# Causal attention sums with the exponentials streaming through column tiles

## The chip, the cores and the metric

The kernel runs on one core of a Trainium2 chip. The metric is the device time of one execution in microseconds. Three timed executions of the kernel before took 1740.86, 1741.07 and 1743.66 us; the median, 1741.07 us, is the time before.

## The reference

Four attention layers follow each other on one sequence of 2048 tokens of width 512, with 32 heads of 16 dimensions: A, B, A, B. Each is added to its input, and each sees its input normalised.

```python
x = A_x
x = x + _A_ref(_layernorm(x), A_wq, A_wk, A_wv, A_wo, A_beta)
x = x + _B_ref(_layernorm(x), B_wqkv, B_wo)
x = x + _A_ref(_layernorm(x), A_wq, A_wk, A_wv, A_wo, A_beta)
x = x + _B_ref(_layernorm(x), B_wqkv, B_wo)
```

Layer A works on four segments of 512 tokens, with a causal softmax inside a segment and a memory carried from segment to segment; layer B is a plain softmax over all 2048 keys.

```python
# A, per segment s
logits = einsum('bhqd,bhkd->bhqk', qs, ks) * scale + mask      # causal, 512 x 512
a_dot = einsum('bhqk,bhkd->bhqd', softmax(logits), vs)
a_mem = (phi(qs) @ M) / (phi(qs) @ z + 1e-6)
o = g * a_mem + (1.0 - g) * a_dot
M, z = M + phi(ks).T @ vs, z + sum(phi(ks))
# B
o = softmax(q @ k.T * Dh ** -0.5) @ v
```

## The kernel before

A Python program writes out the order of all instructions of all engines. It simulates the engines' times as it goes and decides by them what comes next; wherever an engine needs another's result, the semaphore wait is derived from the buffers. The parameters of these decisions are class attributes (how late VectorE may be, how many banks it may take, and so on). `PLAN` overrides some of them for stretches of 40 units each: row k holds for units 40k to 40k + 39.

Layers are numbered 0 to 3; 0 and 2 are causal (A), 1 and 3 bidirectional (B). The attention work is cut into groups. A group is one segment of 512 queries, one chunk `c` of 8 heads, and every second head of it (`e` is 0 or 1), so four heads `r`. The masked queries `qm` hold the query rows of these heads with the others zeroed. Scores are computed transposed, keys on the partitions and queries in the 512 columns of a PSUM bank, in row tiles of 32 partitions that run side by side for the heads.

A causal group has three kinds of banks for each head, `k0`, `k13` and `k2`: the ten blocks of 128 keys by 128 queries on or below the diagonal, packed into whole banks (`PARTS`: key block, first column in the bank, columns, first query). The last kind is a half bank, and the pair's two groups (`e` = 0 and 1) share one bank for it (`k2`, `k2m`). So a pair has 20 banks. The triangle of the diagonal blocks is masked either on PE, by adding a matrix `tri` to the scores, or afterwards on POOL.

A unit takes three banks of scores; ACT exponentiates them together into `pT` (line 1643). Or it takes two, and one or two further banks (a "take", the code's `dx`) go to VectorE, which approximates the exponential in three parts by integer arithmetic: `dx_first` (line 1165) writes the first into `dxt` or into KA, QA, VA, wA or wB where those are idle, `task_dx` and `dx_four` (lines 1219 and 1236) the other two. A take has to be summed over keys three times. `TAKEN` and `TAKEN_A` limit the takes in a group, `REST` asks that so many banks still lie ahead, `R_NEAR`, `R_PAIRS`, `PAIRS` and `ACT1` say when a unit may take one or two; `ring_open`, `dx_open` and `dx_pick` read them.

Two units later the sums over keys follow (`pv_step`, `pv`), into one bank `sums` per group. In a group with `flip`, V of a head (16 columns and a column of ones, which gives the softmax's denominator) is the stationary operand and the 512 exponentials stream; the four heads use four column tiles of 32, so the sums come out with heads and features on the partitions and queries in the columns. Layers 1 and 3 do that, but for the last group. Causal groups have `flip` False: there each 128 x 128 block of exponentials is loaded as the stationary operand and V streams, 17 columns of it (`bcast` repeats them to 34 or 51 so that the write covers the bank), and the sums come out with queries on the partitions.

A group's end differs likewise. `finish` without `flip` takes the reciprocal (line 1732) and multiplies straight from PSUM into `ob` (line 1738). `finish_flip` copies the sums to `ub` (`evac`, line 561, or an addition where sums come in several waves, line 1767), has SP's queue transpose them into `tb`, and after both groups of a pair `divide` takes the reciprocal (line 1784) and multiplies into `ob`, on POOL by default (line 1788). From `ob` the queue transposes into `oT`, and the output projection (`task_out`) reads that. SP issues all transposes in order: `xT` from the normalised input `xn`, `phk` from the keys for the memory, `phq` from `amem`, `tb` and `oT`.

Projections, norms and the memory are background tasks, let in when PE is early against ACT; they use the bank `misc`, which takes use too. `mm_wide` splits a projection's matmul into four column tiles if the current group has `flip`. `keep_busy` and `fill_gaps` add matmuls with zeros (line 2032) where PE would be idle.

Causal groups come first wherever their inputs are ready; in layer 0 two segments can be in work at once, in layer 2 one.

Of the kernel before, what the change touches and what calls it, by code (L numbers as in the profile page):

```python
# [270 lines left out]

class Group:


    __slots__ = ("L", "kind", "qseg", "c", "e", "ksegs", "first", "last", "banks", "pos", "qm", "acc", "npv", "idx", "total", "started", "left", "taken", "shut", "mate", "flip", "begun", "dxr", "bank", "hold")

    def __init__(self, L, kind, qseg, c, e, ksegs, first=True, last=True):
# [22 lines left out]
        self.flip = kind == "B" and (L, qseg, c) != (3, NSEG - 1, NCH - 1)  # L300
        self.left = 40 if kind == "A" else (1 if self.flip else 4) * self.total
# [5 lines left out]
class Builder:  # L307
    STRETCH = 40
    PLAN = {
        0: dict(TAKEN_A=1, MASK_PE=800, PE_LOW=7, GAP=3, BG_BANK=400),  # L310
        1: dict(R_LATE=1200, BUSY_ROOM=300, CARRY_W=0, NEARW=40, PAIRS=999, LEVEL=3, TAKEN=0.5, DVE_LATE=1700, BUSY_BACK=800),
        2: dict(MARGIN=500, DX_BANK=900, NEAR=8, EARLY=300, FILL=0.42, CR_B=1200, PART=3, NEARW=20, PAIRS=60, DX_FIN=3000),
        3: dict(NEAR=8, TAKEN_A=1, PV_SKIP=900, BACK=8, CR_W=1900, NEARW=20, TAKEN=0.4, LOW=14, HOLD_AT=40, PHI_LATE=0),
        4: dict(R_LATE=1200, NEARW=40, PAIRS=24, LEVEL=3, TAKEN=0.5),
        5: dict(DX_LATE=700, SLACK=350, BACK=4, LEVEL=3, BUSY_WAIT=0, PE_LOW=7, DVE_LATE=1700),
        6: dict(NEAR=10, PV_SKIP=200, BACK=3, DX_LAG=3, MASK_PE=800, DIV_LATE=2500, BG_BANK=100, QUAD=0),
        7: dict(REST=10, SLACK=350, R_NEAR=10, EARLY=0, FILL_DVE=200, BUSY_ROOM=300, R_PAIRS=2, PAIRS=999, TAKEN=0.3, QWAIT=8, QMIN=4),
        8: dict(R_LATE=1200, BACK=2, CR_W=1300, NEARW=20, BUSY_WAIT=0, TAKEN=0.3, DVE_LATE=800, QWAIT=3, QMIN=4, HOLD_MAX=0, PHI_LATE=300),
        9: dict(ACT1=400, R_LATE=1200, DX_BANK=700, NEAR=18, CR_W=1900, CR_B=1800, R_PAIRS=2, PAIRS=24, DIV_LATE=800, DVE_LATE=800),
        10: dict(DX_LATE=500, NEAR=5, TAKEN_A=1, SLACK=250, CARRY_W=0, R_PAIRS=2, PAIRS=999, DIV_LATE=800, BUSY_WAIT=0, PE_LOW=4, DVE_LATE=800, BG_BANK=100, QUAD=0, HOLD_MAX=0, PHI_LATE=300),  # L320
        11: dict(DX_LATE=900, R_NEAR=10, BUSY_ROOM=900, FILL=0.42, OPART=4, MASK_PE=800, DIV_LATE=2500, DVE_LATE=800, QWAIT=3, QMIN=4, HOLD_SEGS=2, PHI_LATE=0, POOL_QM=1),
        12: dict(R_LATE=1200, BUSY_ROOM=900, FILL=0.4, OPART=4, LEVEL=3, TAKEN=0.4, DVE_LATE=800, QWAIT=8, QMIN=3, BUSY_BACK=1800),
        13: dict(MARGIN=350, DX_LATE=900, TAKEN_A=1, EARLY=300, CARRY_W=1500, PART=3, OPART=3, MASK_PE=800, GAP=3, QUAD=0, QWAIT=3, HOLD_SEGS=2),
        14: dict(ACT1=400, R_LATE=1200, DX_BANK=700, NEAR=18, CR_W=1900, CR_B=1800, PAIRS=24, DIV_LATE=800, DVE_LATE=800, PHI_LATE=300, DX_FIN=3000),
        15: dict(ACT1=400, MARGIN=400, EVAC_ACT=300, TAKEN_A=2, PV_SKIP=500, BUSY_ROOM=400, CR_A=1700, CARRY_W=400, PART=1, DX_LAG=3, DIV_LATE=800, DVE_LATE=800),
# [764 lines left out]
    def dx_pick(self, used):  # L1090
# [3 lines left out]
        for n, g in enumerate(self.sel):  # L1094
# [5 lines left out]
            for k in sorted(range(1, min(13 if isA else 9, len(g.banks) - g.pos + 1)), key=lambda k: g.dxr[g.banks[-k][1]]):  # L1100
                if g.banks[-k][1] not in used and g.banks[-k][0] != "k2":
                    bank = g.banks.pop(-k)
                    g.taken += 1
                    g.left += (1 if g.flip else 4) * len(EXP_STEPS)
                    g.dxr[bank[1]] += 1
                    for h in self.sel[:n]:
                        h.shut = True
# [989 lines left out]
```

## Time and profile before

| | |
|---|---|
| median of the timed executions | 1741.07 us |
| profiled execution | 1743.75 us, span 1742.0 us |
| instructions | 47805 |
| PE, ACT, VectorE (DVE), POOL busy | 95%, 98%, 88%, 10% of the span |
| mean granted TensorE clock | 0.998 of full |
| bytes moved by DMA | 54.60 MB, mean 31 GB/s |

The profile is one execution. PE's matmuls overlap, and their ends are modelled, so a busy PE isn't PE at its peak; the distance between the starts of matmuls says more. Nearly all matmuls are issued by one helper (line 522), so operands and shapes tell them apart, not lines. In a group's row stand its count, its busy time, the mean duration of one, and the idle time ahead of it with what ended that.

### The profile page before, as it was taken

The numbers are of one execution on the slowest core, as the hardware profiler recorded it, in microseconds if no ns is written. First come the engines' busy times: TensorE is split into PE (matmuls) and PEld (weight loads), VectorE is DVE, ScalarE is ACT, GpSimd is POOL, SyncE is SP. The second block draws the span as 40 slices with busy tenths as digits, with TensorE's granted clock in tenths as the row PEclk, the third lists the DMA queues.
The fourth block names the chain that finished last, engine by engine and source line by source line (L and its number), as shares of the span: only waits on it lengthen the run. The fifth ranks groups of instructions, "written<-read, shape, count | busy, mean of one in ns | idle before, by whom it ended". The sixth has DMA issues, their size and how long they took to land.

```text
span 1742.0 us, 47805 instructions
## 1 busy us (share of the span) xinstructions
PE 1652.7 (95%) x19946; PEld 604.6 (35%) x19946; DVE 1527.2 (88%) x2977; ACT 1703.7 (98%) x1608; POOL 182.8 (10%) x292
## 2 busy tenths in 40 slices
PE   8999899999999899999999999999999999999999
PEld 5553335332222523522235222532222222222236
DVE  6758665999999688799998999889999999999996
ACT  7899999999999999999999999999999999999998
POOL 2310100111100300100002100110010100000000
PEclk9999999999999999999999999999999999999999
DMA  6110211001221221102202111010011001000010
GB/s 176 37 22 20 44 14 29 17 8 22 41 47 23 56 56 32 33 8 59 59 14 38 46 32 41 19 46 14 10 23 26 22 13 23 10 10 11 8 29 18
DMA packets 148440, 54.60 MB, mean 31 GB/s; under 512 B 128768, under 2 KB 147712, under 8 KB 148224
## 3 DMA queue, kind: packets, MB, share of 16 engines
q1 hardware_dynamic: 148224, 51.56, 13.9%
q8 instruction: 156, 2.56, 0.6%
q14 instruction: 60, 0.49, 0.1%
HBM read 18.88 MB, written 2.10 MB: 12 GB/s over the span
## 4 chain that ended last, share of the span: by engine, by line
ACT 43%; PE 36%; issue 11%; DVE 6%; DMA 2%; SPq 1%; POOL 1%; ACTq 0%; DVEq 0%; POOLq 0%
ACT pT L1643 42%; PE ps L522 35%; PE ps L2032 1%; SPq L568 1%; DVE KA L1165 1%; DMA tb<-ub 1%; DMA xT<-xn 1%; POOL pT L1657 1%; DVE dxt L1165 1%; ACT amem L762 0%; DVE wA L1165 0%; DVE lnst L667 0%; POOL qm L1533 0%; DMA phq<-amem 0%; DVE VB L561 0%
## 5 line engine op out<-in xcount | busy, mean ns | idle before, releaser
L1643 ACT ACTIVATE pT<-ps 128x1024 bf16<-128x1024 f32 (+1 forms) x1561 | 1670.8, 1239 | 25.3 <-PE ps L522 19.4
L522 PE MATMUL ps<-qm,KB 32*128 32x512 bf16 x4096 | 571.0, 384 | 56.2 <-ACT pT L1643 43.7
L522 PE MATMUL ps<-pT,VB 128*17 128x512 bf16 x2907 | 497.4, 384 | 1.5 <-DVE QB L561 0.3
L522 PEld LDWEIGHTS ps<-qm,KB 32*128 32x128 bf16 x4096 | 148.4, 91 | 561.0 <-ACT pT L1643 462.0
L1165 DVE TENSOR_SCALAR KA<-ps 128x512 uint16<-128x512 f32 (+1 forms) x453 | 315.3, 704 | 11.4 <-PE ps L522 7.6
L1165 DVE TENSOR_SCALAR dxt<-ps 128x512 uint16<-128x512 f32 (+1 forms) x315 | 220.7, 704 | 12.5 <-PE ps L522 9.7
L522 PEld LDWEIGHTS ps<-pT,VB 128*17 128x17 bf16 x2907 | 116.6, 87 | 287.5 <-issue 274.3
L522 PE MATMUL ps<-dxt,VB 128*17 128x512 bf16 x939 | 197.5, 381 | 0.0
L2032 PE MATMUL ps<-woB,zero 128*32 128x512 bf16 (+7 forms) x655 | 166.9, 295 | 0.0
L522 PE MATMUL ps<-QA,VB 128*17 128x512 bf16 x445 | 129.5, 382 | 0.0
L1165 DVE TENSOR_SCALAR wA<-ps 128x512 uint16<-128x512 f32 (+1 forms) x174 | 123.2, 718 | 3.6 <-PE ps L522 1.1
L1788 POOL TENSOR_TENSOR ob<-tb,rd 128x512 bf16<-128x512 bf16 x31 | 35.7, 1152 | 817.9 <-DVE rd L1784 762.4
L522 PE MATMUL ps<-VA,VB 128*17 128x512 bf16 x445 | 120.3, 381 | 0.0
L1657 POOL TENSOR_SCALAR_AFFINE_SELECT pT<-pT 128x256 bf16<-128x256 bf16 (+4 forms) x113 | 61.7, 561 | 480.8 <-ACT pT L1643 480.8
L522 PE MATMUL ps<-KA,VB 128*17 128x512 bf16 x445 | 109.7, 381 | 0.0
L522 PE MATMUL ps<-wA,VB 128*17 128x512 bf16 x555 | 109.0, 381 | 0.0
L522 PE MATMUL ps<-VA,pT 128*128 128x51 bf16 (+1 forms) x2540 | 104.2, 187 | 4.7 <-POOL pT L1657 2.3
L522 PE MATMUL ps<-qm,KA 32*128 32x128 bf16 (+2 forms) x1536 | 93.1, 255 | 12.8 <-ACT pT L1643 9.4
L522 PEld LDWEIGHTS ps<-VA,pT 128*128 128x128 bf16 x2540 | 89.6, 96 | 23.2 <-issue 7.6
L1533 POOL TENSOR_SCALAR qm<-QB,par 128x512 bf16<-128x512 bf16 x96 | 74.0, 780 | 217.6 <-PE ps L522 197.7
L522 PE MATMUL ps<-woB,zero 128*32 128x512 bf16 (+1 forms) x282 | 92.7, 381 | 0.0
L1165 DVE TENSOR_SCALAR wB<-ps 128x512 uint16<-128x512 f32 (+1 forms) x109 | 81.2, 749 | 3.3 <-PE ps L522 2.4
(165 smaller groups left out, 1979.7 us busy)
## 6 DMA issues: line engine op xcount, KB each, us to landing
wB<-in_B_wqkv_dram SPq DMA_DIRECT2D x48, 128.0 KB, 2.3
wA<-in_A_wk_dram SPq DMA_DIRECT2D x16, 128.0 KB, 2.2
wA<-in_A_wq_dram SPq DMA_DIRECT2D x16, 128.0 KB, 2.4
wA<-in_A_wv_dram SPq DMA_DIRECT2D x16, 128.0 KB, 2.5
out_dram<-x SPq DMA_DIRECT2D x8, 256.0 KB, 2.2
x<-in_A_x_dram SPq DMA_DIRECT2D x3, 512.0 KB, 9.8
wB<-in_B_wqkv_dram SPq DMA_DIRECT2D x1, 1536.0 KB, 12.5
oT<-ob SPq DMA_TRANSPOSE x63, 2.4
```

Source lines behind the costliest of these rows:

```text
L522: self.sc.add("pe", lambda e: e.matmul(out, lhsT, rhs, start=start, stop=stop, skip_group_check=True), reads=reads, banks=[(bank, "w", all ...
L568: t[2] = self.sc.add_dma("sp", lambda e: e.dma_start_transpose(out, in_), b, reads=reads, writes=writes, deps=list(deps) + ([t[2]] if t[2] ...
L1165: self.op("dve", lambda e: e.tensor_scalar(d, o, SCALE * LOG2E * 128, 127.0 * 128 + EXP_BIAS, op0=ALU.mult, op1=ALU.add), writes=[self.b_d ...
L1533: self.op(eng, (lambda m, q, col: lambda e: e.tensor_scalar(m, q, col, 0.0, op0=ALU.mult, op1=ALU.add))(m, q, col), reads=[bq, self.b_par] ...
L1643: self.sc.add("act", (lambda dst, src: lambda e: e.activation(dst, src, ACT.Exp, scale=SCALE))(dst, src), writes=self.b_pT[slot * 3 + i:sl ...
L1657: self.op("pool", (lambda blk, pat: lambda e: e.affine_select(blk, blk, pattern=pat, compare_op=ALU.is_ge, fill=0.0, base=0, channel_multi ...
L1788: self.op(eng, lambda e: e.tensor_tensor(ob, t[:, :, :, 0:16], rb, ALU.mult), reads=[br] + self.b_tb, writes=self.b_ob[oi], **(dict(ns=125 ...
L2032: new = Op("pe", 0, (lambda o, z, w: lambda e: e.matmul(o, z, w, start=False, stop=False, skip_group_check=True))(o, z, w), f"fill {cols} ...
```

## The change

`Group.flip` becomes true for the causal layers in `FLIP_A`, both of them. Their sums run with V stationary and the exponentials streaming, in column tiles. `RUNS` lists for each kind of bank the runs of columns that share a key block and lie side by side in the queries: `k0` is one run of 512, `k13` three (256, 128, 128), `k2` one of 256. So a group has 20 summing matmuls, where it had 40. `pv_step` gathers the banks of one unit that belong to one group, and `pv_many` issues their runs in rounds: the first runs of all heads, then the second runs. `Group.sums` counts the matmuls of a bank. With `flip`, `finish` goes by `finish_flip`, and `mm_wide` and `keep_busy` use column tiles beside causal groups too. All rows of `PLAN` but the last are replaced.

```diff
+FLIP_A = (0, 2)
+RUNS = {"k0": [(0, 0, 512, 0)], "k13": [(1, 0, 256, 128), (1, 384, 128, 384), (3, 256, 128, 384)], "k2": [(2, 0, 256, 256)],
+        "k2m": [(2, 256, 256, 256)]}
...
+    def sums(self, what):
+        if self.kind == "A":
+            return len(RUNS[what]) if self.flip else 2 if what in ("k2", "k2m") else 4
+        return 1 if self.flip else 4
...
-        self.flip = kind == "B" and (L, qseg, c) != (3, NSEG - 1, NCH - 1)
-        self.left = 40 if kind == "A" else (1 if self.flip else 4) * self.total
+        self.flip = L in FLIP_A if kind == "A" else (L, qseg, c) != (3, NSEG - 1, NCH - 1)
+        self.left = sum(self.sums(w) for w in ("k0", "k13", "k2")) * 4 if kind == "A" else self.sums(0) * self.total
...
-        0: dict(TAKEN_A=1, MASK_PE=800, PE_LOW=7, GAP=3, BG_BANK=400),
+        0: dict(DX_LATE=700, DX_BANK=200, SLACK=350, R_NEAR=999, BACK=10, LEVEL=3, BUSY_WAIT=0, PE_LOW=7, DVE_LATE=1700, BG_BANK=400),
...
-        3: dict(NEAR=8, TAKEN_A=1, PV_SKIP=900, BACK=8, CR_W=1900, NEARW=20, TAKEN=0.4, LOW=14, HOLD_AT=40, PHI_LATE=0),
-        4: dict(R_LATE=1200, NEARW=40, PAIRS=24, LEVEL=3, TAKEN=0.5),
-        5: dict(DX_LATE=700, SLACK=350, BACK=4, LEVEL=3, BUSY_WAIT=0, PE_LOW=7, DVE_LATE=1700),
+        3: dict(ACT1=300, R_LATE=1500, REST=4, NEAR=8, TAKEN_A=2, PV_SKIP=900, BACK=8, CR_W=1900, NEARW=20, TAKEN=0.4, LOW=14, HOLD_AT=40, PHI_LATE=0),
+        4: dict(MARGIN=800, R_LATE=1200, SLACK=250, EARLY=0, R_PAIRS=0, NEARW=40, PAIRS=24, LEVEL=1, TAKEN=0.5, LN1_AT=3, POOL_QM=1),
+        5: dict(DX_LATE=700, NEAR=12, SLACK=350, BACK=4, R_PAIRS=2, LEVEL=3, BUSY_WAIT=0, PE_LOW=7, DVE_LATE=1700),
...
-        24: dict(ACT1=200, MARGIN=500, DX_LATE=500, DX_BANK=900, NEAR=8, PV_SKIP=500, FILL=0.42, PART=3, R_PAIRS=0, PAIRS=60, DX_FIN=3000),
+        24: dict(MARGIN=600, DX_LATE=500, EVAC_ACT=300, SLACK=550, PV_SKIP=500, BACK=6, FILL=0.4, CR_B=1200, R_PAIRS=2, MASK_PE=800, DIV_LATE=2500, BUSY_WAIT=500, GAP=1, BG_BANK=100, QWAIT=3, QMIN=3, HOLD_AT=40),
...
+    def pv_many(self, g, ents):
+        what, r, pT, bp = ents[0]
...
         if g.flip:
-            ks, kk = self.kslot(g.L, what // 4), what % 4
-            g.left -= 1
-            self.mm(self.ps[32 * r:32 * r + 17, bank.col0:bank.col0 + 512], self.VB[:, ks, kk, h * 17:(h + 1) * 17], pT,
-                    r not in g.begun, g.left == 0, [bp, self.b_VB[ks][kk]], bank, g.acc, "sumc", tile=(128, 0, 32, 32 * r))
+            todo = []
+            for what, r, pT, bp in ents:
+                h = 8 * g.c + 2 * r + g.e
+                if g.kind == "A":
+                    sl = self.aslot(g.L, g.qseg)
+                    runs = [(off, N, q0, self.VA[:, sl, kb, h * 17:(h + 1) * 17], self.b_VA[sl][kb]) for kb, off, N, q0 in RUNS[what]]
+                else:
+                    ks, kk = self.kslot(g.L, what // 4), what % 4
+                    runs = [(0, 512, 0, self.VB[:, ks, kk, h * 17:(h + 1) * 17], self.b_VB[ks][kk])]
+                todo += [(k, r, pT, bp, run) for k, run in enumerate(runs)]
+                g.npv += 1
+            for k, r, pT, bp, (off, N, q0, v, bv) in sorted(todo, key=lambda t: t[0]):
+                g.left -= 1
+                self.mm(self.ps[32 * r:32 * r + 17, bank.col0 + q0:bank.col0 + q0 + N], v, pT[:, off:off + N],
+                        r not in g.begun, g.left == 0, [bp, bv], bank, g.acc, "sumc", tile=(128, 0, 32, 32 * r), n=N)
+                g.begun.add(r)
             return
...
-            self.pv(g, what, r, self.pT[:, slot, i, :], self.b_pT[slot * 3 + i])
-            used += (r,)
+            ents = [(what, r, self.pT[:, slot, i, :], self.b_pT[slot * 3 + i])]
+            while g.flip and g.kind == "A" and self.pvq and self.pvq[0][:2] == (n, g) and self.pvq[0][4] == slot:
+                _, _, what, r, _, i, _ = self.pvq.pop(0)
+                ents.append((what, r, self.pT[:, slot, i, :], self.b_pT[slot * 3 + i]))
+            self.pv_many(g, ents)
+            used += tuple(e[1] for e in ents)
```

75 lines of the change are left out of this document (37 added, 38 removed).

## The prediction

> **What bounds the kernel now.** I read the page's head first, then the chain.
>
> ```profile
> span 1742.0 us, 47805 instructions
> ...
> PE 1652.7 (95%) x19946; PEld 604.6 (35%) x19946; DVE 1527.2 (88%) x2977; ACT 1703.7 (98%) x1608; POOL 182.8 (10%) x292
> ...
> ACT 43%; PE 36%; issue 11%; DVE 6%; DMA 2%; SPq 1%; POOL 1%; ACTq 0%; DVEq 0%; POOLq 0%
> ```
>
> ACT is busy for 1703.7 of 1742.0 us, VectorE (DVE) for 1527.2: only 38.3 us of ACT's are left to win by filling its idle time. Everything beyond that must shorten ACT's own list of work. The chain changes between ACT and PE because each exponential waits for three score matmuls, and those wait for the bank that an earlier exponential frees. The next question is what ACT's list consists of, and which engine could take some of it. The groups by shape answer that.
>
> ```profile
> L1643 ACT ACTIVATE pT<-ps 128x1024 bf16<-128x1024 f32 x1051 | 1006.0, 1111 | 5.2 <-PE ps L522 3.1
> L1643 ACT ACTIVATE pT<-ps 128x1536 bf16<-128x1536 f32 x510 | 728.1, 1502 | 20.2 <-PE ps L522 16.3 <-POOL pT L1657 1.2 <-POOL VB L923 0.3
> ...
> L1165 DVE TENSOR_SCALAR dxt<-ps 128x512 uint16<-128x512 f32 x303 | 206.1, 684 | 10.0 <-PE ps L522 7.4 <-DVE dxt L1165 0.3
> ...
> L1219 DVE TENSOR_SCALAR dxt<-dxt 128x1024 uint16<-128x1024 uint16 x186 | 76.0, 429 | 0.9
> ```
>
> A step of the program ("unit") exponentiates three banks of scores on ACT (510 times), or two on ACT and one or two on VectorE (1051 times). A bank more in ACT's instruction costs 1502 - 1111 = 391 ns. On VectorE a bank costs 684 ns for its first form and two later forms of 429/2 ns each, 1.11 us together. So the kernel is as long as ACT's list, and the list is shorter the more banks VectorE takes. Where VectorE is not full is seen in the windows (the columns are the window, its length, then busy time and instructions of PE, PEld, DVE, ACT, POOL, the clock, the DMA share, GB/s). Quoted are the windows with causal work of layer 0 (the first three, 174 and 261) and of layer 2 (566, 697, 915, 1089), one between, and one of the bidirectional layers alone.
>
> ```profile
> 0.00:44.00 44.00, 39.00 (x550) 24.53 (x551) 28.64 (x78) 34.76 (x34) 12.39 (x32) 1.00 0.61 175
> 44.00:87.00 43.00, 38.76 (x591) 21.56 (x589) 30.43 (x87) 36.15 (x30) 13.67 (x28) 0.96 0.18 37
> 87.00:131.00 44.00, 41.82 (x642) 22.66 (x640) 24.51 (x53) 42.09 (x34) 6.42 (x14) 1.00 0.11 22
> ...
> 174.00:218.00 44.00, 38.66 (x527) 17.45 (x524) 28.38 (x66) 42.62 (x34) 5.99 (x9) 1.00 0.26 43
> 218.00:261.00 43.00, 39.57 (x450) 13.62 (x454) 27.96 (x55) 42.72 (x35) 1.39 (x2) 1.00 0.10 14
> 261.00:305.00 44.00, 41.73 (x701) 23.36 (x690) 26.02 (x62) 43.61 (x33) 1.19 (x4) 1.00 0.16 29
> ...
> 566.00:610.00 44.00, 39.54 (x669) 23.38 (x673) 28.57 (x71) 43.36 (x36) 15.50 (x25) 1.00 0.22 56
> ...
> 697.00:740.00 43.00, 40.28 (x722) 25.16 (x715) 34.34 (x77) 42.55 (x36) 6.21 (x11) 1.00 0.18 33
> ...
> 915.00:958.00 43.00, 40.28 (x647) 22.28 (x645) 35.64 (x71) 42.68 (x37) 11.25 (x19) 1.00 0.21 39
> ...
> 1089.00:1132.00 43.00, 41.01 (x666) 22.33 (x659) 36.03 (x72) 42.56 (x37) 7.31 (x14) 1.00 0.09 17
> ...
> 1219.00:1263.00 44.00, 42.31 (x430) 12.25 (x427) 43.12 (x81) 43.83 (x47) 3.62 (x4) 1.00 0.05 10
> ```
>
> In 1219 to 1263 all three are full: ACT 43.8, DVE 43.1, PE 42.3 of 44 us, with 47 ACT instructions (two banks each, mostly). In the causal windows ACT is as full, but runs 33 to 37 longer instructions, and VectorE idles: 15.6, 18.0, 15.4, 8.7, 7.4 and 7.0 us in the six after 131, 72 us together. There the work isn't shared out as it is later. Only in the first 131 us does ACT itself idle much: 9.2, 6.9 and 1.9 us.
>
> **The change part by part.** (1) The sums over keys. Of a causal group, 40 matmuls with the exponentials stationary become 20 in which V (17 columns) is stationary and the exponentials stream, each head in its own quarter of the array's columns.
>
> ```profile
> L522 PE MATMUL ps<-VA,pT 128*128 128x51 bf16 x2348 | 103.0, 188 | 4.5 <-POOL pT L1657 2.3 <-DVE ob L1738 1.1 <-DVE amem L857 0.7
> L522 PE MATMUL ps<-VA,pT 128*128 128x34 bf16 x192 | 25.5, 180 | 0.2 <-DVE KA L1165 0.2
> ...
> 191.14 0.50 PE L522 MATMUL ps<-tri,ident 128*128 128x256 bf16 x3
> 191.48 0.47 PE L522 MATMUL ps<-VA,pT 128*128 128x34 bf16 x12
> ...
> 1241.01 0.39 PE L522 MATMUL ps<-qm,KB 32*128 32x512 bf16 x3
> 1241.33 0.39 PE L522 MATMUL ps<-pT,VB 128*17 128x512 bf16 x3
> 1241.34 0.38 PE L522 MATMUL ps<-wA,VB 128*17 128x512 bf16 x1
> 1241.55 0.38 PE L522 MATMUL ps<-dxt,VB 128*17 128x512 bf16 x2
> ```
>
> Now: 12 of them took 0.47 us, the last of them 180 ns (the mean of the 34-column form), so they start (0.47 - 0.18)/11 = 26 ns apart; 2540 (2348 and 192) occupy 67 us. The mean of 188 ns is one matmul's latency, and says nothing of the rate. After: the bidirectional layers already run the new form. Four matmuls of 512 columns on four column tiles start at 1241.33 and 1241.34, the next at 1241.55: 0.21 us for a round of 512 columns. The new runs of one head are 512 + 256 + 128 + 128 + 256 = 1280 columns, so 64 groups of 4 heads stream 327,680; at 0.21 us per 512 that is 134 us, divided by three heads of a unit (45 us) or four (34 us). That saves 22 to 33 us of PE.
>
> Against it stands a switch. At 191.14 three mask matmuls of 256 columns, over the whole array as the sums are, were followed by the sums 0.34 us later: 3 x 256 columns at 0.21/512 are 0.32, so no gap. At 1241.01 scores in row tiles were followed by sums in column tiles after 0.32 us, where the 512 columns take 0.21: 0.11 us lost. With column sums a masked unit pays it once more.
>
> ```profile
> L522 PE MATMUL ps<-tri,ident 128*128 128x256 bf16 x263 | 50.2, 276 | 0.0
> L522 PE MATMUL ps<-tri,ident 128*128 128x128 bf16 x166 | 23.7, 223 | 0.0
> ```
>
> 429 banks (263 and 166) are masked on PE, in threes 143 units: 143 x 0.11 = 16 us. Left are 6 to 17 us of PE time over nine windows of 44 us. I take 11. The Trainium skill would make far more of it: TensorE: Matmul & The Clock Gate, section "Back-to-back issue gap", gives 81 ns for each pair of weight load and matmul at 128 columns in a sustained stream. By that figure the 2540 cost an estimated 206 us, and the change would free about 150 more than reckoned here; the trace disagrees, with 26 ns for a load and a matmul of 34 columns, and the trace decides.
>
> The projections between causal sums go from one 128-wide matmul to four 32-wide ones that run together; at 0.21 us per round either way that is nothing, and their cover is that the column tiles are already in force.
>
> (2) The ends of groups.
>
> ```profile
> L1738 DVE TENSOR_TENSOR ob<-ps,rd 128x256 bf16<-128x256 f32 x66 | 28.0, 424 | 2.3
> L1732 DVE RECIPROCAL rd<-ps 128x16 f32<-128x16 f32 x66 | 16.7, 254 | 32.6 <-PE ps L522 31.8
> L561 DVE CAST ub<-ps 128x512 bf16<-128x512 f32 x36 | 24.5, 680 | 0.0
> L1784 DVE RECIPROCAL rd<-tb 128x32 f32<-128x32 bf16 x31 | 10.7, 345 | 4.1 <-DMA tb<-ub 4.1
> L1788 POOL TENSOR_TENSOR ob<-tb,rd 128x512 bf16<-128x512 bf16 x31 | 35.7, 1152 | 817.9 <-DVE rd L1784 762.4 <-PE ps L522 55.5
> ...
> L568 SPq DMA_TRANSPOSE tb<-ub x62: 1188/1191/2504, 410.6 to 1695.1; - x62
> ...
> DMA to landing us min/median/max: 2.4/2.4/4.4
> ```
>
> Now a pair of causal groups costs VectorE 2 x (254 + 424) = 1356 ns. After, it costs two casts and one reciprocal, 2 x 680 + 345 = 1705, and off VectorE two more transposes on SP (1.19 us of its queue each, 64 in all, ahead of whatever transposes of xT, phk, phq and oT stand behind them) and 1.15 us of POOL. For 32 pairs VectorE gets 32 x 0.35 = 11.2 us more. I put it at nothing: it falls into the windows with 72 us idle. Were they filled, it would push 11.2/1.11 = 10 banks back to ACT, 10 x 0.391 = +3.9 us. The sums bank is read for 680 ns as against 254 + 424, so it comes free no later. Latency is what grows: from the last sum to the normalised tile were 0.68 us, and are 0.68 + 2.4 + 0.34 + 1.15 = 4.6, that is 3.9 more before the oT transpose of the last pair may start. Where other banks are ready that is covered. Where they aren't, the out-projection, the next layer's norm and its first scores are late by it.
>
> (3) The first 131 us.
>
> ```profile
> L522 PE MATMUL ps<-VA,pT 128*128 128x51 bf16 x728 | 31.8, 189 | 0.7 <-DVE ob L1738 0.5
> L522 PE MATMUL ps<-VA,pT 128*128 128x34 bf16 x60 | 7.9, 181 | 0.0
> ...
> ACT pT L1643 <- PE ps L522: 9.5, 17, 1.7
> ...
> 80.00:85.00 5.00, 3.95 (x56) 2.25 (x56) 1.98 (x6) 2.32 (x3) 1.37 (x2) 0.66 0.39 79
> ```
>
> ACT waited 9.5 us here for scores, in 17 waits. Of the causal sums 728 + 60 of the 2540 lie here, 31%, so some 0.31 x 11 = 3.4 us of PE are freed, and at best as much of the 9.5 goes. Three segments end here, and one exposed end takes 3.9 us back. I take zero, with -3.4 and +7.8 (two ends) as its bounds.
>
> (4) The new PLAN rows decide which banks VectorE takes, and when. In the causal stages they go both ways: row 3 (units 120 to 159, the window at 174) lets two causal banks a group be taken (one before) and, of a bidirectional group, asks for 4 banks ahead, not 14; rows 5 and 24 let more single takes queue; rows 0 and 4 cut them. A causal bank on VectorE is summed three times: 3 x 4 x 26 ns = 0.31 us of PE now, 3 x 0.21/3 = 0.21 or less in column tiles, with the fourth tile of a unit of three heads free for it. No row of before shows that mixture. The bounds are nothing moved (0) and half of the 72 us used (36/1.11 = 32 banks, -12.7 us); I take a third, since PE, with 2 to 5 us idle in these windows, must carry them too (22 banks at 0.21 us are 4.6 us, within the 11 freed) and the background work competes for the bank that such a take needs: 24/1.11 = 22 banks, 22 x 0.391 = -8.5 us.
>
> Sum: PE's own saving 0, since outside the start ACT waits for PE hardly at all; ends 0 (+3.9 if uncovered); start 0; banks moved -8.5. The profiled execution took 1743.75 us (span 1742.0) and becomes 1735; the median of the timed runs lies 2.7 below it, 1741.07, and becomes 1732.5.
>
> **The rivals.** First, a longer end shows (slower). The place is 55 to 125 us, where layer 1's first segments depend on layer 0's ends. The window 80 to 85 shows what such a hole costs: ACT 2.3 of 5 us busy and the clock at 0.66. Three segments end there. If each end, and the four phk transposes behind it on SP, comes 3.9 us late while no bank is ready, that is +11.7; with two of three exposed, and none of the 8.5 gained, +7.8: 1749. It decides from the point at which ACT's idle time in 44 to 131 grows beyond the 8.8 us it has now. For it speaks that before layer 1 starts nothing else is ready; against it, that layer 0's next segment usually is. For such a hole the Trainium skill, TensorE: Matmul & The Clock Gate, section "Part 1: The HAM clock gate", gives half the clock after an idle window of about 3.4 us; the row's 0.66 agrees in direction.
>
> Second, nothing moves: ACT's list stays 3632 banks (2 x 1051 + 3 x 510), PE's few microseconds vanish in its slack, the new ends are hidden. Then the time is 1741. For it speaks that ACT waited only 19.4 us in all for scores.
>
> ```profile
> L1643 ACT ACTIVATE pT<-ps 128x1024 bf16<-128x1024 f32 (+1 forms) x1561 | 1670.8, 1239 | 25.3 <-PE ps L522 19.4
> ```
>
> Third, PE was the hidden limit of the causal windows: it is 39 to 42 of 44 us busy there, and background work and VectorE's banks are let in only when PE is early. Then half or more of the idle VectorE time is used, in 218 to 261 (15 us idle) too: (36 + 8)/1.11 = 40 banks, -15.6, and by PE's upper 17 us 0.31 x 17 = 5.3 less at the start: 1720.
>
> **How the numbers follow.** Forecast, 12 to 32 banks moved and a neutral start: 0.50. Late ends: 0.26. Nothing moves: 0.12. Hidden PE limit: 0.12. About 0.2% (3.5 us) is what a measurement of this kernel can tell from no change. Faster: 0.50 + 0.12 = 0.62; same 0.12; slower 0.26. The likeliest case alone spans 1728 to 1737 (32 banks; 22 with the 3.9 us uncovered, or 12). The range runs from the hidden-limit case, 1720, to the middle of the late ends, 1749; left out are the far halves of those two cases, 0.06 and 0.13.
>
> **What would show it.** Right: no 128x51 and 128x34 sums with VA, and some 1280 column-tiled ones with 128 to 512 columns; tb transposes 126, not 62; ACT's 1024-wide instructions up by about 22 and the 1536-wide down; VectorE's idle time in the causal windows down from 72 us by a third; ACT idle before 131 us about 18 us still. Wrong: as many ACT banks as now (then the banks step fails); ACT idle in 44 to 131 above 9 us, with waits for oT, xT or x (then the ends are exposed); PE's sums farther apart than 0.21 us a round, or more than one switch per unit.

## The result and the profile after

The kernel after took 1759.37 us in the median of four runs (1757.08 to 1761.00), the kernel before beside it 1740.99. The ratio is 1.0097, 95% interval 1.0082 to 1.0112: slower by 17 to 18 us, where 8.6 less had been forecast. The profiled execution of after is the fastest of its four (1757.08, span 1755.4), that of before was its slowest, so the spans differ by 13.4 us only. The kernel is 10 lines longer at the helpers and 24 at `divide`, so PE's matmuls are at line 532, the exponential at 1653, the reciprocal of `divide` at 1808 and its product at 1812.

First the page's head, then the two forms of the exponential.

```profile
span 1755.4 us, 47260 instructions
...
PE 1659.6 (95%) x19614; PEld 572.9 (33%) x19620; DVE 1540.3 (88%) x2900; ACT 1704.6 (97%) x1606; POOL 220.7 (13%) x333
...
ACT 41%; PE 28%; DVE 15%; issue 12%; DMA 2%; POOL 1%; SPq 0%; ACTq 0%; DVEq 0%; POOLq 0%
```

```profile
L1653 ACT ACTIVATE pT<-ps 128x1024 bf16<-128x1024 f32 x1027 | 986.6, 1111 | 6.9 <-PE ps L532 5.3 <-ACT pT L1653 0.2
L1653 ACT ACTIVATE pT<-ps 128x1536 bf16<-128x1536 f32 x524 | 750.3, 1498 | 21.0 <-PE ps L532 18.1
```

ACT's own work has hardly changed: 1704.6 us against 1703.7. Its list is 2 x 1027 + 3 x 524 = 3626 banks and one issued alone, 3627 against 3632, and it also copies five groups' sums into `ub` (3.3 us). Its idle time has grown, from 38.3 to 50.8 us. In the chain DVE's share went from 6% to 15%. So on balance next to nothing moved from ACT to VectorE, and the loss is waiting. Where it lies, the windows tell (busy time in the order PE, PEld, DVE, ACT, POOL, then the clock, the DMA share and GB/s).

```profile
44.00:87.00 43.00, 41.44 (x676) 20.48 (x672) 28.67 (x67) 41.62 (x32) 11.30 (x18) 1.00 0.29 51
87.00:131.00 44.00, 36.38 (x365) 13.80 (x364) 24.92 (x57) 32.96 (x30) 8.88 (x14) 0.96 0.23 43
174.00:218.00 44.00, 40.83 (x531) 13.91 (x519) 26.59 (x48) 41.98 (x35) 9.30 (x16) 1.00 0.12 26
...
261.00:305.00 44.00, 42.45 (x630) 19.84 (x625) 26.09 (x55) 43.29 (x33) 15.43 (x21) 1.00 0.30 47
566.00:610.00 44.00, 41.51 (x588) 17.22 (x586) 33.48 (x61) 42.50 (x38) 17.67 (x30) 1.00 0.27 44
697.00:740.00 43.00, 41.00 (x456) 13.24 (x451) 39.63 (x76) 42.93 (x41) 2.55 (x4) 1.00 0.14 29
915.00:958.00 43.00, 41.39 (x461) 14.26 (x455) 41.51 (x79) 42.53 (x45) 5.97 (x10) 1.00 0.10 20
1089.00:1132.00 43.00, 38.88 (x588) 18.78 (x584) 31.76 (x61) 36.85 (x31) 12.01 (x22) 0.96 0.19 34
```

Two windows have holes. In 87 to 131 ACT is busy 32.96 us (before 42.09), in 1089 to 1132 36.85 (before 42.56), and in both the mean granted clock is 0.96. The window 44 to 87 is better than before by 5.5 us (41.62 against 36.15). VectorE's idle time in the six windows after 131 is 17.4, 17.9, 10.5, 3.4, 1.5 and 11.2 us, 62 together, where it was 72. It is a little fuller, with copies from PSUM (70 in these windows, where they were 48) and above all with first forms of exponentials (100 where they were 45).

A window holds other work after than before, so this alone doesn't tell which banks moved. How many causal banks VectorE took in the whole run is read from the sums over keys that read not `pT` but VectorE's results: one row of before, and one of after.

```profile
L522 PE MATMUL ps<-VA,dxt 128*128 128x51 bf16 x48 | 1.9, 187 | 0.0
```

```profile
L532 PE MATMUL ps<-dxt,VA 128*17 128x256 bf16 x27 | 6.4, 276 | 0.0
```

Before, a taken bank has 4 sums in each of its three parts: these 48 and 12 more from KA, QA and VA make 5 banks. After, all are of kind `k13`, with one sum of 256 columns in each part: these 27 and 27 more from KA, QA, VA and wB make 18. So VectorE took 13 causal banks more, and, as ACT's list is only 5 shorter, 8 fewer in the bidirectional layers.

The sums and the ends, by shape, and the masks with what follows them:

```profile
L532 PE MATMUL ps<-pT,VA 128*17 128x256 bf16 x494 | 58.5, 278 | 3.9 <-DVE KA L571 2.0 <-POOL pT L1667 1.0 <-DVE ub L571 0.5
L532 PE MATMUL ps<-pT,VA 128*17 128x512 bf16 x256 | 35.3, 385 | 0.6 <-DVE VB L1787 0.4
L532 PE MATMUL ps<-pT,VA 128*17 128x128 bf16 x476 | 34.8, 220 | 0.0
...
L571 DVE CAST ub<-ps 128x512 bf16<-128x512 f32 x95 | 65.0, 684 | 21.7 <-PE ps L532 21.2
L1808 DVE RECIPROCAL rd<-tb 128x32 f32<-128x32 bf16 x63 | 21.8, 346 | 12.6 <-DMA tb<-ub 12.0 <-issue 0.5
```

```profile
1094.41 0.28 PE L532 MATMUL ps<-tri,ident 128*128 128x256 bf16 x1
1094.63 0.50 PE L532 MATMUL ps<-pT,VA 128*17 128x512 bf16 x7
...
1094.96 0.23 PE L532 MATMUL ps<-pT,VA 128*17 128x128 bf16 x3
...
1095.02 0.22 PE L532 MATMUL ps<-pT,VA 128*17 128x128 bf16 x3
```

These are as foreseen: 1226 sums in column tiles (and the taken banks' beside them), none with V streaming; 95 casts and 63 reciprocals where there were 36 and 31. The switch from a masking matmul to column tiles is there at its price: 256 columns are 0.105 us, the next start is 0.22 us later, so 0.11 lost. Two rounds of 128 columns start 0.06 us apart, about a quarter of the 0.21 us for 512.

The hole in 87 to 131 is followed in the chain (start, duration, what), and in the waits of the whole run (engine and line, what it waited for: us in total, times, longest).

```profile
93.56 4.03 DMA tb<-ub
...
97.67 0.35 DVE rd L1808
98.02 0.55 DVE ub L571
98.57 1.31 DVE xn L705
...
100.52 2.43 DMA xT<-xn
...
103.30 6.83 PE ps L532 x23
```

```profile
DVE rd L1808 <- DMA tb<-ub: 12.0, 10, 3.9
...
PE ps L532 <- DMA xT<-xn: 4.9, 1, 4.9
...
ACT QB L569 <- PE ps L532: 7.3, 1, 7.3
```

A transpose of a causal group's sums lands 4.03 us after its issue, where the median of the 126 is 2.4. It is the fifth of six transposes that SP issued one behind the other from 88.29 to 96.08 us; why it landed late no run shows. VectorE stands at the reciprocal for 3.9 us; behind it in VectorE's order are a cast, the normalised input `xn` of layer 1 and the work on `phk`, so the transpose `xT` is issued at 100.52, PE waits 4.9 us for it, and ACT 7.3 us for the projected queries. That is the first rival's mechanism at its place: a late end ahead of layer 1, with the wait not on the end's own consumers alone but on whatever stands behind the reciprocal on VectorE.

### The profile page after: what moved, and what is told of

Read it like the earlier page. It is cut to its first block, busy times and chain, and to the rows that moved or that the text cites. A ratio compares the mean times of both kernels' runs of the same rounds, so it can differ in the third digit from the quotient of the medians.

```text
span 1755.4 us, 47260 instructions
## 1 busy us (share of the span) xinstructions
PE 1659.6 (95%) x19614; PEld 572.9 (33%) x19620; DVE 1540.3 (88%) x2900; ACT 1704.6 (97%) x1606; POOL 220.7 (13%) x333
## 4 chain that ended last, share of the span: by engine, by line
ACT 41%; PE 28%; DVE 15%; issue 12%; DMA 2%; POOL 1%; SPq 0%; ACTq 0%; DVEq 0%; POOLq 0%
ACT pT L1653 40%; PE ps L532 28%; DVE KA L1175 3%; DMA tb<-ub 2%; DVE dxt L1175 1%; DVE wA L1175 1%; DVE wB L1175 1%; ACT amem L772 1%; PE ps L2060 1%; DVE lnst L677 1%; DVE ub L571 1%; DVE dxt L1229 1%; DVE QA L1229 0%; DMA oT<-ob 0%; DVE VA L1229 0%
## 5 line engine op out<-in xcount | busy, mean ns | idle before, releaser
L1175 DVE TENSOR_SCALAR KA<-ps 128x512 uint16<-128x512 f32 (+1 forms) x413 | 295.1, 721 | 8.0 <-PE ps L532 5.0
L1175 DVE TENSOR_SCALAR dxt<-ps 128x512 uint16<-128x512 f32 (+1 forms) x293 | 204.7, 703 | 9.0 <-PE ps L532 6.5
L532 PE MATMUL ps<-dxt,VB 128*17 128x512 bf16 x855 | 182.4, 381 | 0.0
L1812 POOL TENSOR_TENSOR ob<-tb,rd 128x512 bf16<-128x512 bf16 x59 | 64.4, 1092 | 893.9 <-DVE rd L1808 864.8
L2060 PE MATMUL ps<-woB,zero 128*32 128x512 bf16 (+6 forms) x614 | 156.7, 300 | 0.0
L1175 DVE TENSOR_SCALAR wB<-ps 128x512 uint16<-128x512 f32 (+1 forms) x144 | 109.3, 766 | 3.3 <-PE ps L532 1.7
L532 PE MATMUL ps<-QA,VB 128*17 128x512 bf16 x411 | 110.4, 381 | 0.0
L532 PE MATMUL ps<-wB,VB 128*17 128x512 bf16 x492 | 108.8, 381 | 0.0
L532 PE MATMUL ps<-pT,VA 128*17 128x128 bf16 (+2 forms) x1226 | 92.5, 278 | 4.4 <-DVE KA L571 2.0
L532 PE MATMUL ps<-woB,zero 128*32 128x512 bf16 x296 | 96.3, 381 | 0.2 <-DVE KA L1175 0.2
```

The lines of the kernel that those rows point to most:

```text
L532: self.sc.add("pe", lambda e: e.matmul(out, lhsT, rhs, start=start, stop=stop, skip_group_check=True), reads=reads, banks=[(bank, "w", all ...
L1175: self.op("dve", lambda e: e.tensor_scalar(d, o, SCALE * LOG2E * 128, 127.0 * 128 + EXP_BIAS, op0=ALU.mult, op1=ALU.add), writes=[self.b_d ...
L1812: self.op(eng, lambda e: e.tensor_tensor(ob, t[:, :, :, 0:16], rb, ALU.mult), reads=[br] + self.b_tb, writes=self.b_ob[oi], **(dict(ns=125 ...
L2060: new = Op("pe", 0, (lambda o, z, w: lambda e: e.matmul(o, z, w, start=False, stop=False, skip_group_check=True))(o, z, w), f"fill {cols} ...
```

## The experiments

Two families follow. "In its own order" means that the order of instructions on every engine is the one that the kernel has anyway, and only waits, operands or durations are changed afterwards. The others let the order be planned anew.

**Half of the change.** Four kernels take the code and the PLAN rows apart.

```diff
 plan_only:  FLIP_A = ()      with the rows of after
 flip_only:  FLIP_A = (0, 2)  with the rows of before
 flip_L0:    FLIP_A = (0,)    with the rows of after
 flip_L2:    FLIP_A = (2,)    with the rows of after
```

> The new PLAN rows with the old sums and ends in both causal layers. Late-ends theory (the longer ends by ub, tb and the two reciprocal steps make the new holes in ACT's work): the time is that of the kernel before, 1741, within 4 us, and ACT's idle time in 87 to 131 and 1089 to 1132 is back near 2 and 1 us. PLAN theory (the rows themselves no longer fit): about 1755, with the holes still there. Luck theory (any new order moves the time by some 10 us either way): anywhere from 1735 to 1755.

> The new sums and ends with the old PLAN rows. Late-ends theory: 1755 or more, with VectorE waiting for tb transposes and ACT idle behind it. PLAN theory: 1741 to 1746, since the rows are the old ones and PE is a little freer. Luck theory: no relation to the two others; the sum of the two changes against before need not be +18.

> Column-tile sums and queue ends in layer 0 alone, new PLAN rows. Late-ends theory: about half of the +18 stays, with the hole near 90 to 111 us and none near 1089 to 1132: 1748 to 1753. PLAN theory: as the changed kernel, 1756 to 1760. Luck theory: anywhere in 1740 to 1760.

> Column-tile sums and queue ends in layer 2 alone, new PLAN rows. Late-ends theory: a third to a half of the +18, with a hole in layer 2's last segment and none before 131 us beyond the 9 of before: 1746 to 1752. PLAN theory: 1756 to 1760. Luck theory: anywhere in 1740 to 1760.

Measured: 1810.99 us (ratio 1.0399, interval 1.0367 to 1.0430), 1824.66 (1.0475, 1.0453 to 1.0498), 1796.74 (1.0311, 1.0287 to 1.0335) and 1786.59 (1.0257, 1.0234 to 1.0281). All four are slower than both kernels, by 27 to 84 us, and no expectation came near but the open one for flip_only, "1755 or more". The rows fit one order of work; each of these four kernels, for which they weren't fitted, loses tens of microseconds. So neither half can be priced by itself: averaged over the two sets of rows the column sums cost ((1825 - 1741) + (1759 - 1811))/2 = 16 us and the rows ((1811 - 1741) + (1759 - 1825))/2 = 2, and where code and rows don't belong together (1825 + 1811 - 1741 - 1759)/2 = 68 us come on top. Their traces show one thing more: ACT's list is 3633, 3631, 3633 and 3633 banks, though VectorE idles 253 to 287 us in them (215 before), and though it took 17, 7, 17 and 20 causal banks, counted as above. So the list follows neither; what holds it is not shown.

**Later reciprocals.** After in its own order, but each causal reciprocal stands up to four places later on VectorE where nothing among these needs it, so that the transposes have landed when it comes (115 places in all).

```diff
+            if rd.name == "rdA":
+                while j < i + 4 and ops[j + 1].name != "mulA" and not needs(ops[j + 1], rd):
+                    ops[j] = ops[j + 1]; j += 1
+                ops[j] = rd
```

> The changed kernel with its whole order kept, except that on VectorE each causal reciprocal (the instruction that waits for the tb transposes) stands up to four instructions later, so that the norms, casts and exponential forms behind it don't wait with it (115 such places passed). Stall theory (a large part of the +18 is VectorE standing at that reciprocal while a transpose lands late: 3.9 us at 93.6 and more at 1106, with the two holes in ACT's work behind them): 5 to 9 us less than the changed kernel, 1750 to 1754. Late-x theory (the longer ends make the next layer's inputs late whatever VectorE does meanwhile): 0 to 4 us less, 1755 to 1759.

Measured: 1788.32 us (1.0277, 1.0259 to 1.0295), 29 above after. Both theories expected it to be no slower. Two waits of the whole run:

```profile
DVE oT L1000 <- DMA oT<-ob: 11.8, 6, 4.7
DVE oT L1004 <- DMA oT<-ob: 10.9, 5, 4.2
```

VectorE's wait for `tb` is nearly gone (1.8 us in the whole run, 0.3 before 131), and waits of 23 us for `oT` have taken its place, 4.6 in after; POOL waits 8.4 us for `tb`, in after not at all. The reciprocal is on the path to the output projection: moved back, it makes `oT` later, and VectorE stands there instead. So queueing the reciprocal later did not hide the wait. How the 29 us are made up was not followed further.

**No wait for the transposes.** After in its own order; the causal reciprocals and products read a constant weight tile and don't wait for `tb`. All transposes are still issued. The causal attention's output is not computed.

```diff
+        t = (self.tb if g.kind == "B" else self.woB[:, 0:2, :] ...)
+        for op in self.sc.ops["dve"] + self.sc.ops["pool"]:
+            if op.name in ("rdA", "mulA"):
+                op.deps = [w for w in op.deps if not (w.is_dma and w.name[0] == "tb")]
```

> The changed kernel with its whole order kept, except that the causal ends' reciprocals and products read a constant weight tile in place of tb, so that they wait for no transpose; the transposes are still issued. The causal layers' output is not computed then. Stall theory: 6 to 10 us less than the changed kernel, about 1750. Late-x theory, as far as the order was already laid out for late ends: 2 to 5 us less, about 1755; what remains of the +18 is in the order itself.

Measured: 1751.02 us (1.0053, 1.0040 to 1.0066), 8.3 below after, as the stall theory expected. The stages in which the two differ (first after, then without the wait):

```profile
0.00:131.00 131.00, 116.89 (x1633) 55.29 (x1635) 79.36 (x190) 109.01 (x93) 29.24 (x56) 0.99 0.39 93
1002.00:1176.00 174.00, 163.98 (x2064) 62.83 (x2068) 144.30 (x299) 165.50 (x144) 26.89 (x45) 0.99 0.24 47
```

```profile
0.00:131.00 131.00, 118.41 (x1663) 56.52 (x1665) 79.49 (x193) 112.36 (x96) 29.25 (x56) 1.00 0.43 95
1002.00:1176.00 174.00, 166.35 (x2092) 63.26 (x2089) 146.36 (x306) 167.42 (x145) 27.77 (x46) 0.99 0.23 48
```

Before 131 us ACT gains 3.35 us, in 1002 to 1176 1.9. The wait for `tb` is a cause, and not the whole: 10 us of the 18 between the medians stay.

**Later ends in the kernel before.** Before in its own order; each of the 32 causal `oT` transposes is issued a second time, after the first has landed, and what waits for it waits for the second. SP's queue is held for the first landing too.

```diff
+            if op.name and op.name[0] == "oT" and op.name[1] in (0, 2):
+                new = Op("sp", 0, op.fn, "again")
+                op.deps = op.deps + [new]
+                out.append(new)
```

> The kernel before with its whole order kept, except that each of the 32 causal oT transposes is issued twice, the second after the first has landed: some 2.4 us more at each causal end, and SP waits for it. Late-x theory: the ends lie on the path in layer 0 and in layer 2's single segments, so the time grows by 5 to 12 us, with new holes in ACT's work before 131 us and none elsewhere but in the causal windows. Stall theory: VectorE waits for nothing new, so at most 3 us more.

Measured: 1774.20 us (1.0194, 1.0177 to 1.0210), 33 more, about three times what was expected.

```profile
DVE oT L990 <- DMA oT<-ob: 19.5, 7, 4.6
```

```profile
0.00:131.00 131.00, 112.77 (x1633) 66.15 (x1658) 78.44 (x208) 105.08 (x89) 30.14 (x71) 0.95 0.35 86
```

2.4 us more at each of 32 ends cost 1 us per end on average. VectorE waits 19.5 us for the late `oT`, and ACT is busy 105.08 us of the first 131 (before 113.0, as the rows of the prediction add up) with a clock of 0.95. Before's order does not cover later ends. But the held queue makes other transposes late too: VectorE's wait for `phq` grew from 3.7 to 12.3 us, and the run doesn't separate the two. That after loses less than this, with 3.9 us more per end, fits with an order that was planned with them.

**The same search for four kernels.** Since no set of rows serves two kernels, rows were searched from empty ones against the program's own simulated end, with the same number of trials (about 2290) for four forms: causal sums as before; column sums in both causal layers; column sums in layer 2 alone; column sums in both, with no `tb` transposes issued for them and the causal products on a constant tile (causal output not computed).

```diff
 fit_none:     FLIP_A = ()      PLAN = rows found for it
 fit_flip:     FLIP_A = (0, 2)  PLAN = rows found for it
 fit_flip_L2:  FLIP_A = (2,)    PLAN = rows found for it
 fit_no_tb:    FLIP_A = (0, 2)  no tb in causal layers, PLAN = rows found for it
```

> Causal layers summed as before (FLIP_A empty), with PLAN rows fitted from empty rows by a search of about 2290 trials, the same effort for each of these four kernels, none of which has the rows of before or after. What is compared is the four with each other. Ends theory (the column sums' later ends cost, whatever the rows): this is the fastest, 6 to 16 us below fit_flip. Rows theory (the new sums cost nothing in themselves, after is only fitted less well than before): all four within 4 us of each other.

> Both causal layers in column tiles (FLIP_A = (0, 2)), rows fitted from empty ones with the same effort. Ends theory: 6 to 16 us above fit_none, the more of it before 305 us, where layer 0 runs. Rows theory: within 4 us of fit_none.

> Only layer 2 in column tiles (FLIP_A = (2,)), rows fitted with the same effort. Ends theory: layer 2 has other work ready while its ends are on their way, layer 0 has not, so 0 to 6 us above fit_none and well below fit_flip. Rows theory: within 4 us of both.

> Both causal layers in column tiles, but their tb transposes are not issued and the normalising reads a constant weight tile as soon as the sums are copied (causal attention output not computed); rows fitted with the same effort. Ends theory with the transposes as the cause: at least half of fit_flip's distance to fit_none comes back. Ends theory with the rest as the cause (two casts and a POOL product per pair, sums in column tiles): a third or less comes back. Rows theory: within 4 us of all.

Three or four of the 44 rows that each search found equal rows of before or after.

Measured: 1762.86 us (1.0120, 1.0103 to 1.0137), 1778.78 (1.0209, 1.0194 to 1.0224), 1768.39 (1.0151, 1.0136 to 1.0166) and 1773.85 (1.0183, 1.0166 to 1.0200). The rows theory, all within 4 us, doesn't hold here: with these rows the column sums cost 15.9 us, 10.4 of them by layer 0 and 5.5 by layer 2. Leaving the transposes out gives back 4.9, a third. Where the rest is, the first stage and ACT's list show (fit_none, fit_flip, and of fit_no_tb the stage).

```profile
0.00:131.00 131.00, 117.51 (x1654) 65.47 (x1674) 78.04 (x202) 113.52 (x97) 21.69 (x50) 1.00 0.33 78
L1658 ACT ACTIVATE pT<-ps 128x1024 bf16<-128x1024 f32 x1027 | 984.5, 1108 | 6.9 <-PE ps L537 3.6 <-POOL pT L1672 0.9
L1658 ACT ACTIVATE pT<-ps 128x1536 bf16<-128x1536 f32 x531 | 756.0, 1494 | 18.3 <-PE ps L537 15.4
```

```profile
0.00:131.00 131.00, 114.71 (x1713) 56.11 (x1715) 76.48 (x188) 104.12 (x89) 27.39 (x54) 0.95 0.44 96
L1658 ACT ACTIVATE pT<-ps 128x1024 bf16<-128x1024 f32 x995 | 954.5, 1098 | 6.8 <-PE ps L537 4.4
L1658 ACT ACTIVATE pT<-ps 128x1536 bf16<-128x1536 f32 x561 | 796.2, 1495 | 25.9 <-PE ps L537 21.9 <-ACT pT L1658 0.2
```

```profile
0.00:131.00 131.00, 118.91 (x1655) 56.33 (x1657) 80.23 (x190) 112.48 (x96) 29.96 (x58) 1.00 0.32 78
```

Column sums take 9.4 us of ACT's work out of the first 131 us (104.12 against 113.52, the clock at 0.95), and without the transposes 8.4 of these are back. VectorE waits 7.0 us for `tb` in this stage, up to 5.3 at once, so with rows that are mostly other than those of after the wait for the transposes comes with a hole in the same stage. But ACT's list grew as well: 3648 banks without column sums (2 x 1027 + 3 x 531 and one alone), 3673 with them (2 x 995 + 3 x 561) and 3656 without the transposes (1010 instructions of two banks, 545 of three and one alone); 25 banks at 391 ns are 10 us. 15 of the 25 are causal banks: the rows found without column sums let VectorE take 15 of them, those found with them none. How much of this is the luck of one search, a second one was to tell.

**A second search.** Rows from a second, independent search for the forms without and with column sums.

```diff
 fit_none_2:  FLIP_A = ()      PLAN = rows of the second search
 fit_flip_2:  FLIP_A = (0, 2)  PLAN = rows of the second search
```

> As fit_none (causal layers summed as before), with rows from a second, independent search from empty rows, about 1900 trials. If the 16 us between fit_flip and fit_none were the column sums' doing, this one lies 10 us or more below fit_flip_2, and near the first one's 1762.9. If they were the luck of one search each, the two of the second search lie within 5 us of each other.

> As fit_flip (both causal layers in column tiles), with rows from a second, independent search, about 1900 trials. Column sums' doing: near fit_flip's 1778.8 and 10 us or more above fit_none_2, with the hole in the first 131 us. Luck of the search: within 5 us of fit_none_2, with ACT's list no longer than there.

Measured: 1767.34 us (1.0151, 1.0136 to 1.0165) and 1773.96 (1.0185, 1.0170 to 1.0200), 6.6 us apart: between the two expectations. Each form scatters by about 5 us from one search to the next (1762.9 and 1767.3; 1778.8 and 1774.0), so the 16 of the first search hold some luck; in both the column sums are slower.

```profile
0.00:131.00 131.00, 119.88 (x1697) 65.03 (x1697) 81.00 (x207) 113.68 (x98) 22.47 (x50) 1.00 0.33 80
```

```profile
0.00:131.00 131.00, 114.62 (x1713) 56.45 (x1713) 74.25 (x184) 107.22 (x94) 27.02 (x54) 0.99 0.44 96
...
DVE rd L1838 <- DMA tb<-ub: 26.5, 12, 6.4
```

The hole in the first stage is there again (107.22 us of ACT's work against 113.68), with VectorE waiting 26.5 us for `tb` over the run, up to 6.4 at once, and 11.2 of it in this stage. ACT's list is 3665 banks against 3651, with no causal bank taken in either.

**What else could be the other half.** Three kernels start from the one without the wait (1751.02), again in its own order, and take out one more thing each. The first lets the `oT` transpose read a constant and wait for the casts only, so that the latency from the last sum to its start is that of before; the second copies 384 of 512 columns in the causal casts; the third streams only 32 columns in the sums of 256 and 128. The causal output is not computed in any.

```diff
 no_end_wait:
+                op.deps = [w for w in op.deps if w.name != "mulA"] + ub
 no_tb_cast:
+            k = 384 if g.kind == "A" else 512
+            self.evac(u[:, 0:k], acc[:, 0:k], bu, bank, g.acc)
 no_tb_sums:
+                M = 32 if g.kind == "A" and N < 512 else N
```

> The kernel after in its own order of instructions, with the causal ends' whole latency taken out: the reciprocal and product read a constant weight tile and do not wait for tb, and the oT transpose reads a constant and waits only for the two casts (causal attention output not computed; every instruction and transpose is still issued). From the last sum to the start of the oT transpose it is then 0.68 us, as before the change. Without the tb wait alone it was 1751.0, 10 above before. Latency theory: most of those 10 are the remaining 0.34 + 1.15 us per pair, so 1742 to 1746. VectorE theory (casts and reciprocals delay what stands behind them) or PE theory (the column sums' own time): 1748 to 1751.

> After in its own order, without the tb wait (as in the run before: constant operand, causal output not computed), and the causal casts copy 384 of the 512 columns: about 0.16 us less in each of some 60 casts, 10 us of VectorE, about what the ends added to it. VectorE theory: 3 to 8 us below the 1751.0 of the run without the wait. Latency and PE theories: 0 to 2 us below.

> After in its own order, without the tb wait (causal output not computed), and the causal summing matmuls of 256 and 128 columns stream only 32: of 1280 columns for each head and pair of kinds 640 are left, at 0.21 us per 512 columns and three to four heads side by side 17 to 22 us less of PE. PE theory (the sums in column tiles bound the causal windows): 5 us or more below the 1751.0 of the run without the wait. Latency and VectorE theories: 0 to 3 us below.

Measured: 1751.18 us (1.0049, 1.0036 to 1.0061), 1750.11 (1.0051, 1.0038 to 1.0064) and 1755.10 (1.0065, 1.0051 to 1.0079). None is faster than the 1751.02 by more than the runs of one kernel scatter. For the latency and for VectorE's casts that speaks against their being the other half; the PE theory stays undecided, for a reason given below. The stage in which the kernel without the wait still differs most from before is 1002 to 1176; here before's row, for the one shown above:

```profile
1002.00:1176.00 174.00, 167.57 (x2035) 61.58 (x2034) 156.21 (x308) 172.55 (x159) 19.74 (x34) 1.00 0.14 34
```

ACT is idle 6.6 us there without the wait (174 - 167.42) and 1.45 before; in the profiled executions that is 5.1 of the 5.8 us between the spans (the medians lie 10 apart). What ACT waits for is scores, here in 1045 to 1176, where before has 0.5 us of this:

```profile
ACT pT L1653 <- PE ps L532: 4.7, 10, 1.2
```

VectorE's waits for transposes in the stage are 1.2 us. The stage's mixture differs too: after runs fewer and longer exponentials there (145 ACT instructions against 159), as stages rich in causal work do. So PE is late with scores there; whether by the order of work or by PE's own load was not tried by itself, and none of these runs takes out the switches of tile shape.

The third kernel is a warning. PE had 640 of 1280 columns less to stream, and the time did not fall. But its clock did: three of its five runs, the profiled one among them, had a mean granted clock of 0.989 and took 1755.1 to 1757.0 us, two had 0.995 and took 1750.1 and 1751.6; the run without the wait had 0.998 and 0.999. Carried on to 0.998 by the same slope it would be at about 1748.5 (an estimate), 2 to 3 us below. That is less than the 5 us that the PE theory asks for, but it rests on the slope: this run doesn't decide what the sums' streaming is worth. One of its windows:

```profile
1121.00:1132.00 11.00, 11.00 (x104) 4.35 (x103) 7.43 (x13) 8.96 (x7) 4.08 (x8) 0.50 0.29 60
```

PE is busy all of the 11 us at half the clock, and ACT has 8.96 us of work; in the same window of the run without the wait, whose sums are whole, the clock was 1.00 and ACT full (11.00). There the clock had fallen too, but earlier and for a shorter time.

## Why the prediction was wrong

By its own parts:

- **Sums on PE: right in the prices, the saving not measured.** The 0.11 us of the switch and the rounds are as worked out where they were looked at. The 11 us that they sum to can't be read from PE's busy time, which went from 1652.7 to 1659.6 us and holds matmuls with zeros. That they were worth nothing is not contradicted, but the run with fewer columns leaves it open. The "about 150" beside this sum is 206 - 67 = 139 by its own figures, and it sets a figure for 128 columns against matmuls of 34 and 51, so the trace doesn't contradict that figure.
- **Ends: the step that failed.** The 11.2 us of VectorE were right in size (by the rows of the ends 79.9 us before and 90.9 after, 11.0 more) and rightly put at nothing: some 8 us fewer in the casts (61 of 554 ns, where one took 684) moved the time by 1. The latency was worked out rightly too (2.4 us, 346 ns and 1092 ns measured). But it was put at nothing "where other banks are ready", and priced only for the end of the first segments. It cost 8.3 us, through a way that the text did not name in its part (2): the wait is VectorE's, in order, and `xn`, `phk` and casts stand behind it. The row of 2.4 us in the median was used for it, and the maximum of 4.4 beside it, in the same line, was not; both holes begin with a landing of over 4 us. At the first one the lateness is 1.6 of the 3.9 us that VectorE stood there (an estimate, from 4.03 and 2.4); the other 2.3 would have stayed at the median.
- **Banks moved: failed.** 22 banks were to move from ACT to VectorE, -8.5 us. In the causal layers 13 did (18 taken, where it was 5), but VectorE took 8 fewer in the bidirectional ones. ACT's list became 5 banks shorter, 2 us at 391 ns, and five copies of sums on ACT cost 3.3. What failed is that banks gained in causal windows were priced as banks gained in the whole: in the four mixtures of code and rows the list was the same within two banks, with 7 to 20 causal banks taken and whatever VectorE's idle time. Why, stays open. The condition given ("as many ACT banks as now") is met but for these 5.
- **The first 131 us: failed in size.** Put at 0 with -3.4 and +7.8; ACT's idle time went from 18.0 to 22.0 us, +4, inside these bounds. In 44 to 131, ACT's idle time went from 8.8 to 12.4, above the 9 from which the rival decides.
- **The rivals.** "A longer end shows" is what happened, given 0.26 and 1749 us; by its own price (11.7, with no bank moved) it would have been 1753, and 1759 was measured. It missed the second hole, in layer 2, of the same kind:

```profile
1102.15 4.28 DMA tb<-ub
...
1106.53 0.35 DVE rd L1808
1106.88 1.47 DVE dxt L1229 x2
1108.35 0.61 DVE KA L571
```

A late `tb` again; the reciprocal, two steps of a taken bank and the cast of the keys stand behind it.

From the forecast of 1732.5 us to the measured 1759.4 are 27: 8.5 of banks that did not shorten ACT's work, 8.3 of the wait for `tb`, and some 10 that the prediction had nowhere. For these 10 the rest of the latency and the casts are shown not to be the cause. Not excluded are PE's side (the order of scores and sums, the switches, and the streaming, which the run at the lower clock leaves undecided), the more products on POOL, and the 64 more transposes on SP's queue, which all three of these runs still issue. What is seen is that in 1002 to 1176, the worst stage, ACT waits for PE's scores. The searched rows point to something beside the transposes too: without them column sums stay 11 us slower, with a longer list for ACT, but that is one search, and a form scatters by 5. So the cause of this half stays open. None of the sixteen kernels is faster than the one before.

## What to carry to other kernels

Where an engine executes in order, price a new wait by all that stands behind it on that engine, and by the late landings as well as the median: the line that gave 2.4 us in the median gave 4.4 as the maximum. Idle time of an engine is no capacity by itself: VectorE idled 253 to 287 us in the four mixtures, and ACT's list stayed what it was. Count what moved over the whole kernel and not in the windows where it was to move. And an order that was tuned as a whole has no parts that can be priced alone: with half of a change, or with other rows, it lost 27 to 84 us, so hold the order still and change one wait, operand or size when a cause is to be found.

## What the runs showed of the hardware

A transpose by queue of 128 x 512 landed in 2.4 us in the median and in over 4 us at times (4.03 and 4.28 us at the two holes, 4.5 at most).

The kernel with 640 of 1280 columns of the causal sums left out was no faster, and had the lower clock. In its trace PE was busy for 0.27 us of the microsecond from 1116, and the granted clock was 0.50 from 1120 to 1136. In the run with all columns PE was busy for 0.19 us of the one from 1112, and the clock was 0.50 from 1115 to 1118 only. The Trainium skill, TensorE: Matmul & The Clock Gate, section "Part 1: The HAM clock gate", ties the clock to how busy the array has been; that the fall follows a gap in PE's work in both traces agrees in direction. Why the low clock lasted five times as long with fewer columns, while PE was shown busy, stays open.
